# The first seven steps of a table of complex powers taken from angles and magnitudes, and one doubling step in place

## The chip, the core and the metric

The program runs on one core of one Trainium2 chip. The metric is device time in microseconds (us). Its engines are named as in the profile: PE (TensorE matmul), PEld (TensorE weight load), DVE (VectorE), ACT (ScalarE), POOL (GpSimd) and SP (SyncE, which here issues nearly all DMAs). One kernel computes two independent halves of a result and shares every engine between them.

## The reference

Half A is a Fourier mixing layer on x [2048, 512], with matrices given as inputs. Half B is a long convolution of u [2048, 512] whose taps come from 128 decaying oscillations for each of 512 channels.

```python
a = x @ dft_hid_re.T ; b = x @ dft_hid_im.T
ya = dft_seq_re @ a - dft_seq_im @ b

dt = exp(log_dt)
A = -exp(log_A_real) + 1j * A_imag            # [512, 128]
C = (C_real + 1j * C_imag) * dt[:, None]
P = exp((A * dt[:, None])[:, :, None] * arange(2048))
K = 2.0 * einsum("dn,dnl->dl", C, P).real     # taps, [512, 2048]
yb = causal convolution of u with K along the sequence (by FFTs of length 4096) + u * D_skip
out = concatenate([ya, yb], axis=-1)
```

All of it is float32. The expensive part of B besides the FFTs is P: powers 0 to 2047 of 512 x 128 complex numbers.

## The kernel before

**Order.** A small planner in the kernel file (`Plan`) records the instructions. Each piece of work is a generator that names an engine and an assumed duration before it issues an instruction, and waits for events and counted resources (`Sem`). The planner takes the piece that can start first, then the one of lower "urgency". Its result is one fixed order for each engine; the hardware then only waits on semaphores. A change of assumed durations, urgencies or resources therefore moves instructions on all engines.

**Half A** (`Fnet`) uses the symmetry of the DFT matrices. Four groups t = 0 to 3 of 512 output rows, two parts c each, four tiles k each make 32 loads of 1 MB ("quads", `load_quad`); DVE folds each into `rest` (lines 444 and 449), ACT squares it for a numerical guard (line 473), PE multiplies (`sums`, lines 556 and 559), ACT keeps the sums, and PE makes the second product (`outputs`, lines 655 and 656: four column blocks e of each group, for each of them four k, one f32 and one bf16 matmul of 512 columns, called a pair below). `FNET` holds the urgencies of the four groups; `GROUP_US`, `QUAD_US` and `AHEAD_US` say how early in the plan the loads may begin.

**Half B** (`Ssm`) works in 16 chunks of 32 channels; the 128 partitions are the 128 oscillations. For each chunk two tables are built. The first (`tables1`, tile `t1t`) holds C·A^(64m) for m = 0 to 31. The second (`tables2`, tile `t2`) holds A^l for l = 0 to 31, and `top` holds what stands for l = 32 to 63. PE multiplies both (`taps`, line 1219) into the 2048 taps of each channel. Two chunks make a 64-channel stage of the first FFT step (`stage1_k`). Then, for units of 128, 128, 128, 64 and 64 channels, follow products with the spectrum of u (`product`: line 1461, ACT copies, DVE lines 1491 and 1493, and the matmuls of line 1507) and inverses (`inverse`, line 1578). Intermediate arrays go through DRAM. The last chunk and the last unit have paths of their own (`last_stage1_k`, `last_unit`, lines 1267, 1273, 1476, 1479).

**Seeds.** `seed_args` makes, for one or two chunks at a time (`PAIRS`), the arguments A^(2^j), j = 0 to 10, as magnitudes and angles in the tile `seed` [3, 11, channels]: five copies with a scale on ACT (lines 1046 and 1048), the reduction of the angles on DVE (lines 1050 and 1052), then Abs, Exp and three Sin on ACT with two loads of function tables (lines 1054 to 1062). `seeds` multiplies magnitude with cosine and sine (DVE, line 1072, 704 elements a partition) into `cs`, and ACT adds a copy with signs (line 1078). One `seed` tile exists (`res`, a resource of 1); it is given back when the last chunk's `seeds` has read it.

**Tables.** A table is doubled step by step: `mul` multiplies the rows that are there by a seed (line 997, both real products at once, into a scratch tile `prod` or `prod2`), `add` combines them into new rows (line 1006). In the second table rows 1, 2 and 4 are first copied from `cs` by ACT (lines 1146 and 1149), row 3 comes from row 1 and rows 5 to 7 from rows 1 to 3 (two `mul`, two `add`); even rows from 8 on come from squares (lines 1013, 1026, 1032), odd ones from `mul` and `add`, and `top` from lines 1020, 1167 and 1171. In the first table the last doubling (rows 0 to 15 into 16 to 31) is done by `halves`: `mul` and `add` on the first 16 channels and then on the other 16, because `prod` holds 1024 elements.

## Time and profile before

| | |
|---|---|
| median of 3 runs | 479.33 us (477.11 to 482.01) |
| the profiled execution | 480.8 us, span 479.0 us, mean granted TensorE clock 0.953 |
| PE busy | 398.7 us (83%) |
| DVE busy | 424.7 us (89%) |
| ACT busy | 320.1 us (67%) |
| POOL busy | 1.4 us |
| DMA | 112.52 MB, mean 235 GB/s |

The span is the time from the first to the last instruction of the profiled execution; its own time is 1.8 us more. Rows of a group give a line, an engine, an operation, out<-in with the program's tile names and shapes, the count, then busy us and mean ns of one, then idle time of that engine just ahead of it and what ended it. Rows of the timeline give start, duration, engine, line, operation, tiles, shape and count; where a row stands for several instructions the duration runs from the first start to the last end.

### The profile page before, as it was taken

The page shows a single profiled execution, that of the slowest core. Times are in us where ns is not written, and L with a number is a line of the kernel's source. Part 1 is how long each engine was busy: PE and PEld are TensorE (multiplying, and loading weights), DVE is VectorE, ACT ScalarE, POOL GpSimd, SP SyncE. Part 2 cuts the span into 40 slices and gives each one's busy share as a digit, 9 for nine tenths or more (in the row PEclk, how much of TensorE's full clock was granted, in tenths as well). Part 3 has the DMA queues.
Part 4 walks back from the last instruction along what each step waited for, and adds up shares of the span by engine and source line. Part 5 has one row for each costly group of instructions (what it writes and reads, how often), then busy time and mean ns, then how long its engine had stood idle before and what let it go on. Part 6 is the DMA issues. An engine that isn't in the chain of part 4 may idle for free. (4 is left out here: it accounts for less than half of the span.)

```text
span 479.0 us, 13676 instructions
## 1 busy us (share of the span) xinstructions
PE 398.7 (83%) x5739; PEld 210.9 (44%) x5778; DVE 424.7 (89%) x718; ACT 320.1 (67%) x603; POOL 1.4 (0%) x15
## 2 busy tenths in 40 slices
PE   3669869999987989699898698987988789778593
PEld 3123213435422535264353563544447346456283
DVE  2999998899999998998999999999999999991433
ACT  1537889997796557966798587589748847253231
POOL 0000000000000000000000000000000000000000
PEclk8979879999997999999999999999998999999689
DMA  8995759967888789998867799439462966959575
GB/s 309 387 370 190 249 213 316 322 221 264 229 289 276 273 238 313 296 297 269 252 200 232 246 278 260 110 88 273 133 220 57 272 140 199 242 118 254 187 200 114
DMA packets 128002, 112.52 MB, mean 235 GB/s; under 512 B 53568, under 2 KB 97984, under 8 KB 127424
## 3 DMA queue, kind: packets, MB, share of 16 engines
q1 hardware_dynamic: 119968, 108.58, 74.2%
q10 hardware_dynamic: 7968, 3.02, 2.6%
q8 instruction: 47, 0.77, 0.7%
q14 instruction: 19, 0.16, 0.1%
HBM read 78.09 MB, written 33.49 MB: 233 GB/s over the span
## 5 line engine op out<-in xcount | busy, mean ns | idle before, releaser
L997 DVE TENSOR_TENSOR prod<-tables,cs 128x1024 f32<-128x1024 f32 (+4 forms) x160 | 123.5, 797 | 3.3 <-ACT tables L1146 3.0
L655 PE MATMUL f<-p,w 128*128 128x512 f32 x128 | 68.1, 614 | 6.4 <-ACT y L681 5.2
L1006 DVE TENSOR_TENSOR tables<-prod 128x512 f32<-128x512 f32 (+4 forms) x160 | 72.1, 475 | 0.1
L473 ACT ACTIVATE slots<-rest 128x1536 f32<-128x1536 bf16 x28 | 41.5, 1483 | 17.0 <-DVE rest L444 9.3
L1219 PE MATMUL f<-tables 128*32 128x96 f32 x2048 | 46.3, 247 | 5.1 <-DVE tables L1273 1.4
L444 DVE TENSOR_TENSOR rest<-slots,base 128x512 bf16<-128x512 f32 (+2 forms) x44 | 46.1, 1049 | 3.7 <-DMA slots<-in_sT 2.8
L556 PE MATMUL f<-base,es 128*128 128x512 f32 x64 | 37.1, 664 | 13.9 <-ACT es L357 7.1
L1219 PEld LDWEIGHTS f<-tables 128*32 128x32 f32 x2048 | 42.3, 110 | 12.7 <-issue 6.3
L1171 DVE TENSOR_TENSOR tables<-tables,cs 128x1024 f32<-128x1024 f32 x32 | 38.1, 1219 | 0.0
L655 PEld LDWEIGHTS f<-p,w 128*128 128x128 f32 x128 | 22.6, 191 | 32.1 <-issue 20.9
L556 PE MATMUL f<-base,ec 128*128 128x512 f32 x64 | 35.4, 635 | 0.1
L854 ACT ACTIVATE big<-f 128x512 f32<-128x512 f32 x36 | 20.2, 597 | 15.7 <-PE f L1295 7.9
L1486 ACT ACTIVATE big<-f 128x1024 f32<-128x1024 f32 x24 | 23.6, 1017 | 10.0 <-PE f L1461 9.1
L1461 PE MATMUL f<-big,w 64*32 64x256 f32 (+1 forms) x832 | 24.3, 363 | 7.1 <-DMA big<-xk 5.1
L559 PE MATMUL f<-rest,xi 128*128 128x512 bf16 x86 | 26.6, 402 | 3.8 <-DVE rest L444 2.3
L559 PE MATMUL f<-rest,xr 128*128 128x512 bf16 x87 | 25.7, 390 | 4.2 <-DVE rest L444 2.0
L854 ACT ACTIVATE mid<-f 128x512 f32<-128x512 f32 x24 | 13.0, 591 | 16.2 <-PE f L1507 16.2
L1243 ACT ACTIVATE ks<-f 128x256 f32<-128x256 f32 (+3 forms) x26 | 13.8, 557 | 14.6 <-PE f L1219 14.5
L556 PEld LDWEIGHTS f<-base,es 128*128 128x128 f32 x64 | 11.8, 205 | 26.0 <-ACT es L357 8.1
L1295 PE MATMUL f<-ks,f1k 32*128 32x512 f32 (+1 forms) x224 | 22.5, 527 | 0.1
L1507 PE MATMUL f<-big,ia 32*64 32x256 f32 x384 | 17.5, 409 | 6.1 <-DVE big L1493 3.2
L1461 PEld LDWEIGHTS f<-big,w 64*32 64x32 f32 x832 | 14.9, 106 | 16.6 <-issue 11.0
(191 smaller groups left out, 702.6 us busy)
## 6 DMA issues: line engine op xcount, KB each, us to landing
slots<-in_sT SPq DMA_DIRECT2D x28, 768.0 KB, 7.1
xu<-big SPq DMA_DIRECT2D x16, 512.0 KB, 5.5
base<-in_sT SPq DMA_DIRECT2D x31, 256.0 KB, 6.2
xk<-big SPq DMA_DIRECT2D x6, 1024.0 KB, 7.0
big<-xu SPq DMA_DIRECT2D x12, 512.0 KB, 7.2
big<-xk SPq DMA_DIRECT2D x12, 512.0 KB, 7.6
zs<-mid SPq DMA_DIRECT2D x10, 512.0 KB, 5.4
big<-zs SPq DMA_DIRECT2D x10, 512.0 KB, 5.7
```

Source lines behind the costliest of these rows:

```text
L444: return v.tensor_tensor(rest[:, lo:hi:step], raw[:, lo:hi:step], base[:, None, :].to_broadcast([128, n, DM]), op=op)
L473: nc.scalar.activation(raw, rest, AF.Square, accum_out=self.stat[:, n:n + 1])
L556: nc.tensor.matmul(out, x[:, cols], base, start=k == 0, stop=False)
L559: nc.tensor.matmul(out, still[:, cols], rest[:, h], start=False, stop=k == 3 and h == 2)
L655: nc.tensor.matmul(ps, self.w[k][:, cols], self.p[t, c][:, d], start=k == 0, stop=False)
L854: self.nc.scalar.activation(to, src, AF.Copy)
L997: self.nc.vector.tensor_tensor(p.rearrange("p k d c m -> p k (d c) m"), src.rearrange("p d c l -> p (d c) l")[:, None, :, rows].to_broadca ...
L1006: self.nc.vector.tensor_tensor(dst[:, :, :, rows], p[:, 0], p[:, 1, :, ::-1], op=OP.add)
L1171: self.nc.vector.tensor_tensor(self.top[:, :, k, ::1 - 2 * k, 16:32], t[:, :, :, 1:32:2], cs[:, k, 5, :, :, None].to_broadcast([128, CHUNK ...
L1219: nc.tensor.matmul(ps[32 * j:32 * j + 32, i], t1[:, d, c], t2[:, :, d, c], start=c == 0, stop=c == 1, tile_position=(0, 32 * j))
L1461: nc.tensor.matmul(both[:, :, c], self.w2[rows, R * q + r, xx, 32 * c:32 * c + 32], xs[rows, r, xx], start=True, stop=True, tile_position= ...
L1486: a.activation(flat[:, 1024 * m:1024 * m + 1024], p.rearrange("p b d -> p (b d)"), AF.Copy)
```

## The change

The angles and magnitudes are made for fifteen powers instead of eleven: 1 to 7 and then 8, 16, ... 1024, and the tile `seed` is turned round to [3, channels, 15], so that the fifteen values of one channel lie side by side. A new process `direct` multiplies magnitude by cosine and sine for the powers 1 to 7 straight into rows 1 to 7 of the second table (one DVE instruction of 448 elements). The ACT copies into rows 1, 2 and 4 and the two `mul` and two `add` that made rows 3 and 5 to 7 are gone. `seeds` now makes the eight powers from 8 on (512 elements instead of 704), and reads them across the channels, 15 elements apart. `seed_args` issues nine scaled copies on ACT instead of five (`POWERS`), and its other instructions cover 15 values a channel instead of 11.

The resource `res` becomes two halves of the tile; it is given back when both the `seeds` and the `direct` of all its chunks have read it (`took_seeds`). The groups are now chunk 0, chunk 1, and then seven pairs, instead of chunk 0, seven pairs, and chunk 15.

The last doubling of the first table is done by `in_place` for all chunks but the last: one product into `prod` (1024 elements), one product straight into the new rows (1024), one addition in place (1024), instead of two products of 1024 and two additions of 512.

Three planner constants differ: `FNET` 2.0 becomes 1.5 for all groups, `GROUP_US` 29 becomes 37, `AHEAD_US` 35 becomes 15.

```diff
-        self.kss, self.res = Sem(1), Sem(1)
+        self.kss, self.res = Sem(1), Sem(2)
...
+    def in_place(self, name, t, rows, seed, to, between=()):
+        d, m = t.shape[1], len(range(64)[rows])
+        n = 2 * d * m
+        p = self.tab.tile([128, 1024], F32, name=name)[:, :n].rearrange("p (d c m) -> p d c m", d=d, c=2)
+        for k, out in ((1, p), (0, t[:, :, :, to])):
+            yield "dve", dve(n), *APART[:2 * bool(between or not k)]
+            self.nc.vector.tensor_tensor(out, t[:, :, :, rows], seed[:, k, :, :, None].to_broadcast([128, d, 2, m]),
+                                         op=OP.mult)
+        yield from between
+        yield "dve", dve(n), *APART[:2 * bool(between)]
+        self.nc.vector.tensor_tensor(t[:, :, :, to], t[:, :, :, to], p[:, :, ::-1], op=OP.add)
...
-        yield self.res
-        s = self.tab.tile([128, 3, 11, 2 * CHUNK], F32, name="seed")[:, :, :, :w]
+        for _ in range(PAIRS[g][1]):
+            yield self.res
+        o = CHUNK if g == 1 else 0
+        s = self.tab.tile([128, 3, 2 * CHUNK, 15], F32, name="seed")[:, :, o:o + w]
...
-        a.activation(args[:, :, 0], par[:, 0:2], AF.Copy)
-        for j in (1, 2, 4, 8):
-            a.activation(args[:, :, j:min(2 * j, 11)], args[:, :, 0:min(j, 11 - j)], AF.Copy, scale=2.0 ** j)
-        yield "dve", dve(n, 2)
+        for steps in POWERS:
+            yield "act", sum(0.1 + 2 * w * len(range(15)[to]) * 0.00083 for to, _, _ in steps) + 0.09
+            for to, of, scale in steps:
+                a.activation(args[:, :, :, to], par[:, 0:2, :, None] if of is None else args[:, :, :, of], AF.Copy,
+                             scale=scale)
+        n = 15 * w
...
+    def took_seeds(self, g):
+        self.seeds_left[g] -= 1
+        if not self.seeds_left[g]:
+            for _ in range(PAIRS[g][1]):
+                self.plan.put(self.res)
+
     def seeds(self, g, j, s):
         yield self.css
-        s = s[:, :, :, CHUNK * j:CHUNK * j + CHUNK]
-        cs = self.tab.tile([128, 2, 11, CHUNK, 2], F32, name="cs", bufs=2)
-        yield "dve", dve(22 * CHUNK)
-        self.nc.vector.tensor_tensor(cs[:, :, :, :, 0], s[:, 1:3], s[:, 0:1].to_broadcast([128, 2, 11, CHUNK]),
+        s = s[:, :, CHUNK * j:CHUNK * j + CHUNK, 7:].rearrange("p n d l -> p n l d")
+        cs = self.tab.tile([128, 2, 8, CHUNK, 2], F32, name="cs", bufs=2)
+        yield "dve", dve(16 * CHUNK)
+        self.nc.vector.tensor_tensor(cs[:, :, :, :, 0], s[:, 1:3], s[:, 0:1].to_broadcast([128, 2, 8, CHUNK]),
...
-            yield from self.halves("prod", t, slice(0, 16), cs[:, :, 10], slice(16, 32), n == 15 and self.t1_half)
+            if n == 15:
+                yield from self.halves("prod", t, slice(0, 16), cs[:, :, 7], slice(16, 32), self.t1_half)
+            else:
+                yield from self.in_place("prod", t, slice(0, 16), cs[:, :, 7], slice(16, 32))
...
+    def direct(self):
+        for n in range(16):
+            yield "urgency", 2 + FIRST_TABLE * n + DIRECT
+            yield self.box_ev[n]
+            yield self.lent_ev
+            yield self.t2s
+            if n == 15:
+                self.plan.spawn(self.last_unit(), 1)
+            g, j, seeds = self.box.pop(n)
+            seeds = seeds[:, :, CHUNK * j:CHUNK * j + CHUNK, :7]
+            yield "dve", dve(14 * CHUNK)
+            self.nc.vector.tensor_tensor(self.t2[n % 2][:, :, :, 1:8].rearrange("p d c l -> p c d l"), seeds[:, 1:3],
+                                         seeds[:, 0:1].to_broadcast([128, 2, CHUNK, 7]), op=OP.mult)
+            self.took_seeds(g)
+            self.plan.set(self.low_steps[n])
...
             yield self.cs_ev[n]
-            yield self.lent_ev
-            yield self.t2s
+            yield self.low_steps[n]
...
-            yield "act", act(2 * CHUNK), ahead
-            a.activation(t[:, :, :, 1].rearrange("p d c -> p c d"), cs[:, :, 0, :, 0], AF.Copy)
-            for c in range(2):
-                yield "act", act(2 * CHUNK), ahead
-                a.activation(t[:, :, c, 2:6:2].rearrange("p d j -> p j d"), cs[:, c, 1:3, :, 0], AF.Copy)
-            p = yield from self.mul("prod2", t, slice(1, 2), cs[:, :, 1])
-            yield from self.add(p, t, slice(3, 4))
-            p = yield from self.mul("prod2", t, slice(1, 4), cs[:, :, 2])
-            yield from self.add(p, t, slice(5, 8))
...
-PAIRS = ((0, 1), *((n, 2) for n in range(1, 15, 2)), (15, 1))
+PAIRS = ((0, 1), (1, 1), *((n, 2) for n in range(2, 16, 2)))
-FNET, GUARD, XTS = (2.0, 2.0, 2.0, 2.0), 2, 2
+FNET, GUARD, XTS = (1.5, 1.5, 1.5, 1.5), 2, 2
-GROUP_US, QUAD_US, AHEAD_US = 29, 7.0, 35
+GROUP_US, QUAD_US, AHEAD_US = 37, 7.0, 15
```

What this does to the order is shown at three places. In the rows below, a name such as prod_2833 is the scratch tile of the second table, prod without a number that of the first; the line numbers of the changed program are 13 to 41 higher from `in_place` on (L1006 became L1019, L1072 L1095, L1171 L1207, L1461 L1497, L1491 L1527, L1578 L1614).

DVE before, in the middle of the program: the end of the tenth chunk's second table (L1167, L1171) and the first seeds that are read from a newly filled `seed` tile (L1072, for the twelfth chunk). The reduction of the angles of that group's tile (L1052) stands eight rows ahead of the first row shown.

```order
L1032 TENSOR_TENSOR tables<-square 128x32x4
L1006 TENSOR_TENSOR tables<-prod_2833 128x64x4
L997 TENSOR_TENSOR prod_2852<-tables,cs 128x1024
L1026 SCALAR_TENSOR_TENSOR tables<-tables 128x32x8
L1032 TENSOR_TENSOR tables<-square 128x32x8
L1006 TENSOR_TENSOR tables<-prod_2852 128x64x8
L1167 SCALAR_TENSOR_TENSOR tables<-tables 128x32x16
L1171 TENSOR_TENSOR tables<-tables,cs 128x64x16
L1171 TENSOR_TENSOR tables<-tables,cs 128x32x2x16
L997 TENSOR_TENSOR prod<-tables,cs 128x128
L1072 TENSOR_TENSOR cs<-seed 128x704
```

DVE now, also at the end of the tenth chunk's tables, which is the turn to a new pair: the reduction of the new pair's angles (L1068), the last rows of the tenth chunk, and the first instruction that reads the new seeds, the direct product of the eleventh chunk (L1178).

```order
L1068 TENSOR_TENSOR seed<-seed 128x960
L1019 TENSOR_TENSOR tables<-prod 128x64x8
L1039 SCALAR_TENSOR_TENSOR tables<-tables 128x32x8
L1010 TENSOR_TENSOR prod<-tables,cs 128x1024
L1010 TENSOR_TENSOR tables<-tables,cs 128x64x16
L1045 TENSOR_TENSOR tables<-square 128x32x8
L1014 TENSOR_TENSOR tables<-tables,prod 128x64x16
L1019 TENSOR_TENSOR tables<-prod_2594 128x64x8
L1203 SCALAR_TENSOR_TENSOR tables<-tables 128x32x16
L1207 TENSOR_TENSOR tables<-tables,cs 128x64x16
L1207 TENSOR_TENSOR tables<-tables,cs 128x32x2x16
L1178 TENSOR_TENSOR tables<-seed 128x2x32x7
```

Between the reduced angles and the first instruction that reads the finished tile there were seventeen rows, and there are ten now; the tile's next filling begins only after the last L1178 of its chunks.

DVE before, behind the last table row of the last chunk (the second L1171): products of the third and fourth unit (L1491, L1493), and the transposes (L1273) that empty the PSUM banks of the last chunks' first FFT step.

```order
L1171 TENSOR_TENSOR tables<-tables,cs 128x32x2x16
L1491 TENSOR_TENSOR slots<-big_105 128x512
L1493 TENSOR_TENSOR big_105<-big_105 128x2x256
L1491 TENSOR_TENSOR mid_108<-slots 128x512
L1273 STREAM_TRANSPOSE tables<-f_4518 128x2x8x32
```

DVE now, at the same place.

```order
L1207 TENSOR_TENSOR tables<-tables,cs 128x32x2x16
L1527 TENSOR_TENSOR mid_108<-big_107 128x512
L1309 STREAM_TRANSPOSE tables<-f_4280 128x2x8x32
L1529 TENSOR_TENSOR big_107<-big_107 128x2x256
L1309 STREAM_TRANSPOSE tables<-f_4284 128x2x8x32
```

One product row stands ahead of the first transpose instead of three.

PE before, directly ahead of the last chunk's taps: a product of the third unit (L1461, 2x128), the last pair of half A's output (L655, L656) and the first product of the fourth unit (2x64); behind the taps PE has no more work of half A.

```order
L1461 MATMUL f_4455<-big_105,w_98 32x2x128 x16
L1461 MATMUL f_4456<-big_105,w_98 32x2x128 x16
L655 MATMUL f_4253<-p_3169,w_518 128x512
L656 LDWEIGHTS v_551
L656 MATMUL f_4253<-low_3360,v_551 128x512
L1461 MATMUL f_4498<-slots,w_98 32x2x64 x32
```

PE now, behind the last chunk's taps: inverse pieces of the second unit (L1614), both products of the fourth unit (L1497, two rows each), and the first of eight pairs of half A's last two output blocks.

```order
L1614 MATMUL f_4468<-big_105,ib 64x128 x8
L1497 MATMUL f_4470<-big_106,w_98 32x2x64 x32
L1497 MATMUL f_4505<-big_106,w_98 32x2x64 x32
L1614 MATMUL f_4468<-big_105,ib 64x128 x8
L655 MATMUL f_4508<-p_3643,w_245 128x512
L656 LDWEIGHTS v_387
L656 MATMUL f_4508<-low_3722,v_387 128x512
L1497 MATMUL f_4586<-tables,w_98 32x2x64 x32
L1497 MATMUL f_4597<-tables,w_98 32x2x64 x32
L655 MATMUL f_4508<-p_3643,w_410 128x512
```

Behind the last taps there stood three 64-channel products (L1461), five double groups of L1507 and eight groups of L1578; now there are four, five and twelve, and the eight pairs of half A, spread between the products and groups of the last two units.

39 lines of the change are left out of this document (23 added, 16 removed).

## Prediction

> **What bounds the kernel now.** I read the page's busy times first, then the busy time by stage, then who waited for whom on DVE. The chain of waits is of no use here: it ends after one instruction of 0.1%.
>
> ```profile
> PE 398.7 (83%) x5739; PEld 210.9 (44%) x5778; DVE 424.7 (89%) x718; ACT 320.1 (67%) x603; POOL 1.4 (0%) x15
> DVE  2999998899999998998999999999999999991433
> ```
>
> The digits show DVE near full from the second to the 36th of 40 slices and mostly idle in the last four. So the kernel has two parts, and the stages are cut at the end of the last table row on DVE, the end of the last taps on PE, and the last matmul:
>
> ```profile
> core 0: us, PE busy (x) PEld busy (x) DVE busy (x) ACT busy (x) POOL busy (x), PEclk, DMA share, GB/s
> 12.00:425.68 413.68, 358.21 (x4623) 178.96 (x4664) 399.43 (x684) 302.58 (x573) 0.53 (x1) 0.96 0.78 239
> 432.33:474.17 41.84, 31.64 (x936) 24.07 (x936) 15.47 (x20) 13.51 (x23) 0.00 (x0) 0.88 0.72 196
> ```
>
> Up to 425.68 us DVE works 399.43 of 413.68 us: what it saves there comes off, as long as nothing makes it wait. From 432.33 to 474.17 it works 15.47 of 41.84 us; there PE is the busiest, with 31.64 us and 10.2 us idle. DVE's waits in the first part are few:
>
> ```profile
> DVE prod L997 <- ACT tables L1146: 3.0, 3, 1.7
> DVE rest L444 <- DMA slots<-in_sT: 2.8, 4, 1.3
> ```
>
> **What an instruction costs DVE.** The groups by shape give durations, the timeline gives starts:
>
> ```profile
> L997 DVE TENSOR_TENSOR prod<-tables,cs 128x1024 f32<-128x1024 f32 x64 | 77.5, 1217 | 0.1
> L1006 DVE TENSOR_TENSOR tables<-prod 128x512 f32<-128x512 f32 x64 | 43.7, 683 | 0.0
> L997 DVE TENSOR_TENSOR prod<-tables,cs 128x128 f32<-128x128 f32 x32 | 11.9, 379 | 3.0 <-ACT tables L1146 3.0
> L1006 DVE TENSOR_TENSOR tables<-prod 128x128 f32<-128x128 f32 x16 | 4.6, 288 | 0.1
> L997 DVE TENSOR_TENSOR prod<-tables,cs 128x384 f32<-128x384 f32 x16 | 8.9, 554 | 0.0
> L1006 DVE TENSOR_TENSOR tables<-prod 128x192 f32<-128x192 f32 x16 | 5.6, 352 | 0.0
> L1052 DVE TENSOR_TENSOR seed<-seed 128x704 f32<-128x704 f32 x7 | 6.2, 883 | 0.0
> L1050 DVE TENSOR_SCALAR seed<-seed 128x704 f32<-128x704 f32 x7 | 3.7, 522 | 0.0
> ...
> 299.26 0.89 DVE L1072 TENSOR_TENSOR cs<-seed 128x704 f32<-128x704 f32 x1
> 300.06 0.28 DVE L1006 TENSOR_TENSOR tables<-prod 128x64 f32<-128x64 f32 x1
> 300.19 0.72 DVE L997 TENSOR_TENSOR prod<-tables,cs 128x128 f32<-128x128 f32 x2
> 300.83 0.42 DVE L1006 TENSOR_TENSOR tables<-prod 128x64 f32<-128x64 f32 x2
> ...
> 321.26 2.35 DVE L1171 TENSOR_TENSOR tables<-tables,cs 128x1024 f32<-128x1024 f32 x2
> 323.53 0.37 DVE L997 TENSOR_TENSOR prod<-tables,cs 128x128 f32<-128x128 f32 x1
> ```
>
> Between 1024 and 512 elements the duration falls by 534 ns: 1.04 ns an element. Two of 1024 start 1.135 us apart (323.53 less 321.26, halved), 0.08 us less than one lasts, so an instruction takes its elements' time and 0.07 us. By that the 512 take 0.60 us, the 704 0.80 (300.06 less 299.26), the 384 0.47, the 192 0.27, the 64 0.13, and a 128 of line 997 0.32 (0.64 for two).
>
> **The change on DVE, part by part.** For each chunk the two products and two additions of rows 3 and 5 to 7 go: 0.32 + 0.13 + 0.47 + 0.27 = 1.19 us, 19.0 us for 16 chunks. The seeds fall from 704 to 512 elements: 0.20 us, 3.2 us in all. The direct product of 448 elements costs 0.07 + 0.47 = 0.54 us, 8.6 us in all. The angle reduction grows from 704 to 960 elements for a pair: 0.27 us for the subtraction, and 0.13 us for the rounding, which runs at two elements in that time (522 ns for 704); 0.40 us for seven pairs and half of it for two single chunks are 3.2 us. The last doubling takes three instructions of 1.135 instead of two of 1.135 and two of 0.60: 0.06 us less, 15 times, 0.9 us. Together 11.3 us less.
>
> The trace does not show the new reading of the seeds: both operands step 15 elements (60 bytes) from one to the next. One end is no excess: line 1072 now writes 8 bytes apart and its 0.80 us is 704 elements at the usual rate. The nearest row in kind is the 128-element product of line 997, which reads one element of each 32-element table row, 128 bytes apart: 379 ns against 288 for an addition of 128, 0.71 ns an element more. For 512 elements that is 0.36 us, 5.8 us in all; 11.7 us if both operands pay one after the other; 0 if that row pays for its inner length of one, not for the distance. I take half of 5.8, 2.9 us, because the row allows either reading, and keep 0 and 11.7 for the range.
>
> [...]
>
> **Waits.** The three ACT copies into the table go, and with them 3.0 us of DVE waiting. What can take their place is the seed chain:
>
> ```profile
> 330.26 0.89 DVE L1052 TENSOR_TENSOR seed<-seed 128x704 f32<-128x704 f32 x1
> 331.24 0.79 ACT L1054 ACTIVATE seed<-seed 128x704 f32<-128x704 f32 x1 [0.70 <-DVE seed L1052]
> 336.54 0.87 ACT L1062 ACTIVATE seed<-seed,halfpi 128x704 f32<-128x704 f32 x1
> ```
>
> From 331.24 to 337.41 ACT needs 6.2 us; 256 more elements in each of four steps add about 0.9 us, as 704 take 0.8. The tile is now held until the direct product of the pair's second chunk, so the next filling starts later: ten DVE rows stand behind the reduction in the place shown, some 8 us by the prices above, where seventeen stood. 7.1 us and ACT's other work in between leave next to nothing. I take 0.4 us of waiting for each of seven pairs, 3 us, between 0 and 8. It cancels the 3.0.
>
> DVE therefore ends its tables 11.3 - 2.9 = 8.4 us earlier. The taps behind them follow 1.2 us closer: they waited for a transpose ahead of which three 512-element products stood, and now one, 0.60 us each. Their end moves from 432.3 to 422.7 us.
>
> **The end of the program.** The order now puts behind the last taps what PE had done before them:
>
> ```profile
> 417.71 0.38 PE L656 MATMUL f<-low,v 128*128 128x512 bf16 x1
> 418.79 0.38 PE L656 MATMUL f<-low,v 128*128 128x512 bf16 x1
> 446.59 1.90 PE L1461 MATMUL f<-tables,w 64*32 64x128 f32 x94 [3.42 <-issue]
> 456.83 2.55 PE L1461 MATMUL f<-tables,w 64*32 64x128 f32 x128
> 459.32 1.09 PE L1578 MATMUL f<-tables,ib 128*64 128x128 f32 x16
> 471.18 1.15 PE L1578 MATMUL f<-tables 128*64 128x64 f32 x32 [1.69 <-issue]
> 473.02 1.15 PE L1578 MATMUL f<-tables 128*64 128x64 f32 x32 [0.69 <-ACT tables L854]
> ```
>
> Eight pairs of half A at 1.08 us (418.79 less 417.71) are 8.6 us, one more 64-channel product 2.5, four more inverse groups at 1.09 are 4.4: 15.5 us more PE work, added to 31.64. Against that stand PE's 10.2 us idle, of which 3.4 are the one gap ahead of 446.59. The pairs lie just there, between products, and are long matmuls; the idle time near the end (1.69 us before 471.18, 0.69 before 473.02) has nothing to fill it. I take 7.1 of the 10.2 us as filled: this part grows by 8.4 us, between 5.3 (all filled) and 15.5 (none).
>
> **Sum.** -8.4 (DVE) - 1.2 (taps) + 8.4 (end) = -1.2 us. In the second table an addition and the product behind it more seldom stand next to each other now that four short dependent steps are gone; I count 0 for it, up to 2 us less. The profiled execution's 480.8 us become 479.6; it lies 1.5 us above the median of the runs, so 478.1 us. With the up to 2 us at half, 477 us.
>
> **Rivals.** Results within about 1% (474.5 to 484.1 us) cannot be told from no change here.
>
> *Forecast*, the end gives back most of what DVE saves: 477, own range 472 to 481. For it speaks the order at the end, against it that PE's pairs may fill more. Chance 0.43.
>
> *The saving stays.* Strided reading costs nothing, the seed chain keeps clear and all of PE's idle time is filled: 479.3 - 11.3 - 3.0 - 1.2 - 2 + 5.3 = 467 us. For it speaks that all removed instructions lie where DVE is full; with one of the three missing it is 470 to 473. Chance 0.31.
>
> *The end grows by its full work.* PE's idle time is "issue", not lack of work; if each short product brings its own gap as before 446.59, the end grows 15.5 us: 477 + 7.1 = 484 us. It ends slower than before as soon as that stretch grows by more than 10.7 us. Chance 0.16.
>
> [...] Chance 0.10. [...]
>
> **Range and chances.** Faster by over 1%: 0.28 of the second case and 0.11 of the first, 0.39. Slower by over 1%: 0.08 of the third, 0.07 of the fourth, 0.15, and 0.02 of the first. Within 1%: 0.44. From 467 to 485 us about 2 in 10 are left out.
>
> **What would show it.** Line 1095's 512 elements at 684 ns: free; near 1.05 us: one operand pays; 1.4: both. Idle time ahead of lines 1066, 1095 and 1178 is the seed chain. The last row of line 1207 should start near 416 us, and the last taps end near 423. PE from there to its last matmul should take 50 us with 47 busy. If that stretch stays near 42 us, or the last table row comes after 422 us, the prediction is wrong in that step.

## The result, and the profile after

The changed kernel takes 484.82 us (median of 12 runs, 480.20 to 489.57), the kernel before, run beside it, 479.00 (12 runs, 477.11 to 483.08). The ratio is 1.0119, with a 95% interval of 1.0083 to 1.0154: slower by 1.2%, some 5.7 us. The forecast was 477.0, no change or a little faster; the time lies at the upper end of its range of 467 to 485. The profiled execution took 486.56 us, with a span of 484.8. In the experiments E5, E9 and E11 the profiled execution was one of that kernel's longer ones, so the lengths of its stages are not used.

First the busy times and the DVE digits of the page after, which answer to those of before (DVE 424.7 us in 718 instructions):

```profile
span 484.8 us, 13631 instructions
PE 405.9 (84%) x5778; PEld 212.0 (44%) x5778; DVE 417.0 (86%) x655; ACT 330.7 (68%) x591; POOL 1.4 (0%) x15
DVE  3999998899999998999899999999999997934260
```

DVE has 7.7 us less to do, PE 7.2 us more busy time, and the span is 5.8 us longer. The busy time by stage of the changed kernel, cut at the end of the last table row on DVE, the end of the last taps and the last matmul as before:

```profile
core 0: us, PE busy (x) PEld busy (x) DVE busy (x) ACT busy (x) POOL busy (x), PEclk, DMA share, GB/s
12.00:420.86 408.86, 350.25 (x4446) 171.36 (x4448) 390.25 (x617) 308.43 (x554) 0.53 (x1) 0.94 0.74 232
427.38:479.47 52.09, 46.22 (x1152) 32.45 (x1152) 18.62 (x26) 18.28 (x30) 0.00 (x0) 0.93 0.86 231
```

The first stage ends 4.8 us earlier than before (420.86 for 425.68), the last taps 4.95 us earlier (427.38 for 432.33). The stretch behind them takes 52.09 us instead of 41.84: PE works 14.6 us more there and is idle 5.9 us instead of 10.2. So in this pair of executions the first stage gains 4.8 us, and the end takes twice as much back.

The instructions of the change, by shape:

```profile
L1095 DVE TENSOR_TENSOR cs<-seed 128x512 f32<-128x512 f32 x16 | 16.9, 1056 | 0.2 <-ACT seed L1078 0.2
L1178 DVE TENSOR_TENSOR tables<-seed 128x448 f32<-128x448 f32 x16 | 9.9, 617 | 1.9 <-ACT seed L1078 1.9
L1068 DVE TENSOR_TENSOR seed<-seed 128x960 f32<-128x960 f32 x7 | 8.1, 1151 | 0.0
L1066 DVE TENSOR_SCALAR seed<-seed 128x960 f32<-128x960 f32 x7 | 4.6, 657 | 3.1 <-ACT seed L1062 3.1
```

The direct product and the angle reduction cost what was worked out. The seeds of line 1095 take 1056 ns where 512 neighbouring elements take 684: 0.37 us more each, 6.0 us in all.

The longest waits that are new or grown (engine and line, for whom; us in total, times, longest), of DVE and of PE:

```profile
DVE tables L1045 <- ACT square L1026: 5.2, 4, 2.4
DVE seed L1066 <- ACT seed L1062: 3.6, 6, 1.0
...
PE f L1255 <- DVE tables L1207: 9.5, 1, 9.5
```

DVE's waits for ACT up to the last table row add up to 12.6 us where they were 6.0. PE stands 9.5 us ahead of the taps of the sixth chunk, which the new order puts in its queue before their table is done.

Last, the rows on PE in the last stretch that the experiments turn on, and its busy time in two slices of 4 us there:

```profile
436.53 1.09 PE L1614 MATMUL f<-big,ib 128*64 128x128 f32 x14
439.71 0.38 PE L1614 MATMUL f<-big,ib 128*64 128x128 f32 x2 [2.09 <-issue]
440.02 1.58 PE L655 MATMUL f<-p,w 128*128 128x512 f32 x2
441.96 3.37 PE L1497 MATMUL f<-tables,w 64*32 64x128 f32 x128
...
445.25 1.12 PE L655 MATMUL f<-p,w 128*128 128x512 f32 x2
450.78 2.03 PE L1497 MATMUL f<-tables,w 64*32 64x128 f32 x128
```

```profile
436.00:440.00 4.00, 1.91 (x59) 1.31 (x45) 2.68 (x4) 1.72 (x2) 0.00 (x0) 1.00 0.94 209
440.00:444.00 4.00, 4.00 (x84) 2.48 (x90) 0.00 (x0) 0.60 (x1) 0.00 (x0) 0.57 1.12 265
```

In the middle of a group of 16 like matmuls PE stops for 2.09 us and waits for nothing that the profile shows. In the 4 us after that the granted clock is 0.57, and the next product takes 3.37 us where the same product later takes 2.03.

### The profile page after: what moved, and what is told of

Same layout as the page of the kernel before. It is cut to its first block, busy times and chain, and to the rows that moved or that the text cites. A ratio compares the mean times of both kernels' runs of the same rounds, so it can differ in the third digit from the quotient of the medians.

```text
span 484.8 us, 13631 instructions
## 1 busy us (share of the span) xinstructions
PE 405.9 (84%) x5778; PEld 212.0 (44%) x5778; DVE 417.0 (86%) x655; ACT 330.7 (68%) x591; POOL 1.4 (0%) x15
## 5 line engine op out<-in xcount | busy, mean ns | idle before, releaser
L655 PE MATMUL f<-p,w 128*128 128x512 f32 x128 | 70.1, 630 | 6.8 <-ACT y L681 6.8
L997 DVE TENSOR_TENSOR prod<-tables,cs 128x1024 f32<-128x1024 f32 (+3 forms) x98 | 74.3, 774 | 1.7 <-ACT cs L1100 1.2
L1255 PE MATMUL f<-tables 128*32 128x96 f32 x2048 | 49.4, 255 | 13.8 <-DVE tables L1207 9.5
L1255 PEld LDWEIGHTS f<-tables 128*32 128x32 f32 x2048 | 45.3, 114 | 23.1 <-issue 11.8
L1019 DVE TENSOR_TENSOR tables<-prod 128x256 f32<-128x256 f32 (+3 forms) x98 | 44.0, 463 | 0.0
L1207 DVE TENSOR_TENSOR tables<-tables,cs 128x1024 f32<-128x1024 f32 x32 | 38.3, 1218 | 0.0
L655 PEld LDWEIGHTS f<-p,w 128*128 128x128 f32 x128 | 22.3, 193 | 32.3 <-issue 19.1
L559 PE MATMUL f<-rest,xi 128*128 128x512 bf16 x96 | 28.7, 407 | 1.8 <-DVE xi L273 1.0
L1062 ACT ACTIVATE seed<-seed 128x128 f32<-128x128 f32 (+2 forms) x72 | 28.0, 456 | 0.9
L1497 PE MATMUL f<-big,w 64*32 64x256 f32 (+1 forms) x832 | 25.1, 369 | 3.4 <-DMA big<-xk 1.4
L1026 ACT ACTIVATE square<-tables 128x256 f32<-128x256 f32 (+1 forms) x32 | 16.5, 517 | 14.8 <-DVE tables L1178 11.4
L656 PE MATMUL f<-low,v 128*128 128x512 bf16 x64 | 24.8, 387 | 0.0
L593 PE MATMUL f<-base,bec 128*128 128x512 bf16 x32 | 13.7, 504 | 12.5 <-ACT p L619 11.5
L559 PEld LDWEIGHTS <-xi 128*128 128x128 bf16 x96 | 9.7, 102 | 28.1 <-issue 23.3
```

The lines of the kernel that those rows point to most:

```text
L559: nc.tensor.matmul(out, still[:, cols], rest[:, h], start=False, stop=k == 3 and h == 2)
L655: nc.tensor.matmul(ps, self.w[k][:, cols], self.p[t, c][:, d], start=k == 0, stop=False)
L997: self.nc.vector.tensor_tensor(p.rearrange("p k d c m -> p k (d c) m"), src.rearrange("p d c l -> p (d c) l")[:, None, :, rows].to_broadca ...
L1019: self.nc.vector.tensor_tensor(dst[:, :, :, rows], p[:, 0], p[:, 1, :, ::-1], op=OP.add)
L1062: a.activation(args[:, :, :, to], par[:, 0:2, :, None] if of is None else args[:, :, :, of], AF.Copy, scale=scale)
L1207: self.nc.vector.tensor_tensor(self.top[:, :, k, ::1 - 2 * k, 16:32], t[:, :, :, 1:32:2], cs[:, k, 2, :, :, None].to_broadcast([128, CHUNK ...
```

## The experiments

Ratios are against the kernel before, run beside each, with 95% intervals; 1% is 4.8 us. The stage rows below are cut at the start of the last table row, at the end of the last taps and at the end of the last matmul.

### E1: the old planning numbers

```diff
-FNET, GUARD, XTS = (1.5, 1.5, 1.5, 1.5), 2, 2
+FNET, GUARD, XTS = (2.0, 2.0, 2.0, 2.0), 2, 2
-GROUP_US, QUAD_US, AHEAD_US = 37, 7.0, 15
+GROUP_US, QUAD_US, AHEAD_US = 29, 7.0, 35
```

> The changed kernel with the three planning numbers of before (2.0, 29 and 35 in place of 1.5, 37 and 15); all work is done. Theory A (the loss lies in what stands behind the last taps, and it is the shorter DVE work, not these numbers, that moves work there): the order still puts eight pairs of half A and 288 product matmuls behind the last taps, so the last table row starts near 420 us, the stretch from the last taps to the last matmul stays between 50 and 54 us, and the time between 481 and 488 us. Rival B (the new planning numbers are at fault): the stretch falls back towards 42 us and the time to 474 to 478 us.

Measured: 492.09 us, ratio 1.0238 (1.0154 to 1.0322). The last table row starts at 417.62 us, the last stretch takes 56.72. Rival B falls: with the old numbers the changed kernel is slower still. The stretch and the time are longer even than Theory A had them (50 to 54 us, 481 to 488).

### E2: the higher seeds side by side by channel

```diff
+        low = args[:, :, :7 * w].rearrange("p n (d l) -> p n l d", l=7)
+        high = args[:, :, 7 * w:].rearrange("p n (l d) -> p n l d", d=w)
...
-        s = s[:, :, CHUNK * j:CHUNK * j + CHUNK, 7:].rearrange("p n d l -> p n l d")
+        s = s[:, :, 7 * w:].rearrange("p n (l d) -> p n l d", d=w)[:, :, :, CHUNK * j:CHUNK * j + CHUNK]
```

> The changed kernel, its order on DVE and PE unchanged row for row, with the eight higher powers of a seed tile stored power by power, so that line 1095's product reads neighbouring elements; the seven low powers stay side by side for each channel; all work is done. Theory A (strided reading costs 0.37 us a seed product, and DVE's end sets the start of the last stretch): the seed product falls from 1056 ns to about 684, the 16 of them by 6.0 us, the last table row starts near 414 us instead of 419.65, the last stretch stays near 52 us, and the time falls by 5 to 6 us to about 479. Rival C (PE, behind with its own work, sets the end whatever DVE does): the last table row starts earlier but the stretch behind grows by the same, and the time falls by less than 2 us. Rival D (the seed's ACT work comes late now): idle time ahead of the seed products takes up half of it or more, and the time is 481 to 483.

Measured: 481.79 us, ratio 1.0082 (1.0028 to 1.0136). The seed product's group, DVE's longest wait, and the first and last stage of this kernel:

```profile
L1100 DVE TENSOR_TENSOR cs<-seed 128x512 f32<-128x512 f32 x16 | 11.1, 691 | 0.0
...
DVE seed L1070 <- ACT seed L1067: 6.1, 7, 1.4
```

```profile
12.00:417.49 405.49, 343.79 (x4363) 173.18 (x4409) 383.53 (x617) 308.74 (x552) 0.52 (x1) 0.94 0.74 233
425.66:477.80 52.14, 44.59 (x1147) 31.53 (x1152) 18.67 (x26) 18.27 (x30) 0.00 (x0) 0.93 0.87 229
```

The stride is the whole price: 691 ns instead of 1056, 5.8 us off DVE. But the ratio falls only from 1.0119 to 1.0082, 1.8 us (3.0 by the medians), and the two intervals overlap. Something else moved too: ACT's copies into the new layout became dearer (23 of them take 572 ns instead of 496), and DVE's wait for them ahead of the rounding (line 1070, 1066 in the changed kernel) grew from 3.6 to 6.1 us. In the first stage DVE is busy for 5.5 us less and idle for 3.4 us more. That is Rival D in part, one step earlier than it said: nothing waits ahead of the seed products themselves. The stretch behind the last taps stays where it was, 52.14 us, so Rival C's mechanism is not seen, although the fall of the ratio is of its size.

### E3: the late pairs left out

```diff
                 cols = slice(128 * e, 128 * e + 128)
+                if t == 3 and e > 1:
+                    if k == 0:
+                        nc.tensor.matmul(ps, self.w[k][:, cols], self.p[t, c][:, d], start=True, stop=True)
+                    continue
```

> The changed kernel without 15 of the 16 matmuls of the eight pairs of half A that stand behind the last taps (of the last 512 rows, the output's last two blocks of 128 columns: their first matmul stays); nothing else moves. Theory A (that stretch is bound by PE, and the pairs lie on its path): 15 matmuls at about 0.57 us are 8.5 us of PE work; the stretch falls from 52.1 to 44 to 47 us and the time to 477 to 479 us. Rival E (the pairs fill time in which PE would wait anyway, and the stretch is long for another reason): PE's busy time there falls by 8.5 us but its idle time grows by 6 or more, and the time stays between 482 and 485 us.

Measured: 483.12 us, ratio 1.0043 (1.0005 to 1.0080). The last stretch, and three of the rows on PE in it:

```profile
423.28:474.05 50.77, 38.91 (x1133) 28.00 (x1132) 18.73 (x26) 18.05 (x30) 0.00 (x0) 0.97 0.89 236
```

```profile
437.14 0.38 PE L1618 MATMUL f<-big,ib 128*64 128x128 f32 x2 [2.92 <-issue]
442.06 0.41 PE L1501 MATMUL f<-tables,w 64*32 64x128 f32 x4 [1.56 <-issue]
447.92 1.29 PE L1501 MATMUL f<-tables,w 64*32 64x128 f32 x69 [2.50 <-issue]
```

The edit leaves one matmul of each of the two blocks, so 14 of the 16 are gone. PE's busy time in the stretch falls by 7.3 us, the stretch by 1.3; PE's unexplained stops grow instead, inside groups of like matmuls. Over all runs the kernel is 1.7 us (medians) to 3.6 us (ratios, whose intervals just part) shorter than the changed one. So Rival E is right in the main: the pairs cost the end a half of their length at most. (Up to the last taps this kernel issues the same instructions as the changed one, yet its last table row started at 415.65 us instead of 419.65: single executions differ by that much, which is why stages are compared here only where the difference is larger or is repeated.)

### E4: the order of a slower DVE

```diff
-            yield "dve", dve(14 * CHUNK)
+            yield "dve", dve(14 * CHUNK) + 1.0
```

> The changed kernel, with the planner told that the direct product of each chunk takes 1.0 us longer than it does (16 us in all, about what the change takes off DVE); every instruction is the same, only the order differs: behind the last taps stand one pair instead of eight, 128 product matmuls instead of 256 and 96 inverse matmuls instead of 128. Theory A (the saving is real and is given back by the order at the end): the last table row starts near 420 us as in the changed kernel, the stretch behind the last taps takes 38 to 43 us with some 30 busy, and the time is 471 to 476 us, under the kernel before. Rival C (PE has no room before the last taps, so that pulling its work ahead of them makes the taps late by the same): the last taps end near 432 us or later and the time stays at 480 to 485 us.

Measured: 489.95 us, ratio 1.0177 (1.0112 to 1.0241). Its three stages:

```profile
12.00:433.51 421.51, 359.94 (x4660) 179.24 (x4699) 394.84 (x624) 314.24 (x562) 0.53 (x1) 0.94 0.77 237
433.51:448.05 14.54, 13.62 (x314) 8.73 (x315) 5.84 (x8) 3.09 (x5) 0.00 (x0) 1.00 0.73 201
448.05:486.24 38.19, 27.14 (x746) 21.67 (x747) 13.11 (x17) 10.88 (x20) 0.00 (x0) 0.88 0.59 153
```

The end is as short as ordered, 38.19 us. But the work that was pulled ahead of the taps makes them 20 us later: the last table row starts at 433.51, with DVE idle for 26.7 of 421.5 us, and PE is busy for nearly all of the 14.5 us behind it. Theory A in its first form falls with this run: in this order, at least, moving PE's work forward does not bring the saving. It is Rival C's mechanism, at a time beyond its range; the 3 us by which the ratio exceeds that of the changed kernel are within the intervals.

### E5, E9, E10, E14, E15: one engine after the other relieved, in the order of before

E5 leaves out the two products and two additions whose removal is the heart of the change, and moves nothing else. E9 leaves out PE work, E10 both, E15 adds ACT to E5, E14 relieves all three.

```diff
(DVE)
-            p = yield from self.mul("prod2", t, slice(1, 2), cs[:, :, 1])
-            yield from self.add(p, t, slice(3, 4))
-            p = yield from self.mul("prod2", t, slice(1, 4), cs[:, :, 2])
-            yield from self.add(p, t, slice(5, 8))
+            for n4 in (128, 64, 384, 192):
+                yield "dve", dve(n4)
(PE)
+                if t < 3 and e < 3 and k in (1, 2):
+                    continue
(ACT)
-        nc.scalar.activation(raw, rest, AF.Square, accum_out=self.stat[:, n:n + 1])
+        nc.scalar.activation(raw[:, 0, :128], rest[:, 0, :128], AF.Square, accum_out=self.stat[:, n:n + 1])
```

> The kernel before, its order unchanged row for row, without the two products and two additions that make rows 3 and 5 to 7 of each chunk's second table (those rows hold zeros, set once by GpSimd); the ACT copies into the table stay. That takes 1.19 us a chunk, 19.0 us in all, off DVE and moves nothing on PE. Theory A (DVE sets the table stage, and only the changed order loses the gain): the last table row starts near 407 us instead of 424, the last stretch stays near 42 us, and the time falls to 460 to 465 us. Rival C (PE has hardly any room before the last taps, so that DVE is not alone in setting the stage): DVE's new idle time is spent waiting for PE, for buffers that PE frees or for half A's steps, the last table row comes at 416 us or later, and the time is 471 to 477 us.

> The kernel before, order unchanged, without 18 of half A's output pairs (of the first three groups of 512 rows, the first three blocks of 128 columns: the two middle ones of four pairs each); all of them stand in the table stage, and 18 at 1.08 us are 19.4 us off PE; DVE keeps all its work. Theory C (PE and DVE bind the table stage together, each waiting now and then for the other): the last table row comes 2 to 6 us earlier and the time is 473 to 477 us. Rival A (DVE alone binds it): within 2 us of the kernel before.

> Both reliefs at once in the order of the kernel before: 19.0 us off DVE (rows 3 and 5 to 7 of the second tables left at zero) and 19.4 us off PE (the same 18 pairs left out). Theory C: what the one engine alone could not turn into time now comes through; the time falls by 13 to 19 us, more than the two reliefs alone together, to 461 to 468 us. Rival I (a third thing holds the stage, the transfers or the in-order queues themselves): no more than the sum of the two alone, 470 us or more.

> The kernel before, order unchanged, with 19.0 us off DVE (rows 3 and 5 to 7 of the second tables at zero), 19.4 us off PE (18 output pairs of half A left out) and now some 34 us off ACT (the guard's sums over 128 columns). Theory K: with the third engine relieved the 19 us come through, and the time falls to 458 to 466 us. Rival L: no more than 3 us below the 473 us of the two reliefs.

> The kernel before, order unchanged, with 19.0 us off DVE and some 34 us off ACT, PE untouched. Theory K with PE as the next bound: between the 475 us of DVE's relief alone and 466 us. Rival L: 473 to 477 us, as with DVE's relief alone.

| run | taken off, as priced | ratio | interval |
|---|---|---|---|
| E5 | DVE 19.0 us | 0.9854 | 0.9769 to 0.9939 |
| E9 | PE 19.4 | 0.9938 | 0.9897 to 0.9978 |
| E10 | DVE 19.0, PE 19.4 | 0.9845 | 0.9777 to 0.9914 |
| E15 | DVE 19.0, ACT 34 | 0.9879 | 0.9822 to 0.9935 |
| E14 | all three | 0.9888 | 0.9832 to 0.9943 |

With DVE relieved the kernel gains 1.1 to 1.6%, some 5 to 7.5 us, whatever else is relieved. E5's Theory A (460 to 465 us) falls; its 475.24 us are Rival C's. E9, PE relieved alone, gains 0.6%, some 3 us, a little more than its Rival A allowed. The stage up to the last table row, in E10, E14 and E15 in this order (before: 412.45 us long, PE busy 358.03 at clock 0.96, DVE 398.20):

```profile
12.00:421.11 409.11, 351.76 (x4604) 177.60 (x4602) 384.55 (x618) 300.65 (x571) 1.41 (x3) 0.92 0.77 241
```

```profile
12.00:420.58 408.58, 349.19 (x4567) 177.65 (x4602) 384.59 (x619) 265.20 (x571) 1.41 (x3) 0.92 0.78 241
```

```profile
12.00:419.44 407.44, 357.76 (x4619) 178.05 (x4656) 385.19 (x618) 265.25 (x571) 1.41 (x3) 0.95 0.78 242
```

Three things can be read. Of the 19.0 us priced, 13 to 13.7 arrive as less DVE busy time. The traces show why: most DVE instructions start 0.08 us before the one ahead has ended, but in the kernel before 54 of the stage's 682 start right behind its end, and in E10, E14 and E15 108 to 110 do. The new ones are nearly all an addition behind its own product, or a product behind the addition whose rows it reads: the instructions left out had stood between them. Some 55 times 0.08 us are 4.4 of the missing 5.3 to 6 us. Second, only 3.3 to 5 us of those 13 shorten the stage; DVE's idle time grows from 14.2 to between 22 and 25 us. (The rest of E10's gain lies in its last stretch, 36.90 us, whose instructions are those of before: the stages of single executions differ by several us, the ratios of whole runs are the firmer figure.) Third, PE's relief was given back through the granted clock. E14 and E15 differ by PE's relief alone: 19.4 us less work take 8.6 us off PE's busy time (357.76 to 349.19), and 357.76 less 19.4 is 338.4 us at 0.95, which at 0.92 is 349. What lowers the clock the runs do not show; in the last stretch of the changed kernel a stop of 2.09 us stood ahead of the 4 us at 0.57.

Theory C of E10 and Theory K fall: beside DVE's relief, 19.4 us off PE and 34 us off ACT change nothing that can be measured. Rival I stands: DVE's relief brings what it brings alone, and neither PE nor ACT is what holds the rest back.

### E7 and E8: the new numbers alone, the doubling alone

```diff
(E7, kernel before)
-FNET, GUARD, XTS = (2.0, 2.0, 2.0, 2.0), 2, 2
+FNET, GUARD, XTS = (1.5, 1.5, 1.5, 1.5), 2, 2
-GROUP_US, QUAD_US, AHEAD_US = 29, 7.0, 35
+GROUP_US, QUAD_US, AHEAD_US = 37, 7.0, 15
(E8, kernel before)
-            yield from self.halves("prod", t, slice(0, 16), cs[:, :, 10], slice(16, 32), n == 15 and self.t1_half)
+            if n == 15:
+                yield from self.halves("prod", t, slice(0, 16), cs[:, :, 10], slice(16, 32), self.t1_half)
+            else:
+                yield from self.in_place("prod", t, slice(0, 16), cs[:, :, 10], slice(16, 32))
```

> The kernel before with the three planning numbers of the changed one (1.5, 37 and 15); all work is done. The order behind the last taps keeps its counts (no pair of half A, 192 product and 96 inverse matmuls). Theory A and rival C alike (the numbers are not what loses): within 4 us of the kernel before. Rival B (the numbers are at fault): 483 us or more.

> The kernel before with one part of the change alone: the last doubling of the first table in place (three instructions of 1024 elements instead of two of 1024 and two of 512, 15 times); all work is done. On DVE that is 0.9 us less. Because the planner works out the order anew, behind the last taps now stand 256 product and 128 matmuls of the next step instead of 192 and 160. Theory A: 477 to 480 us. Rival H (any renewed order moves the time by several us, whatever the edit saves): more than 3 us away from the kernel before, in either direction.

Measured: E7 481.96 us, ratio 1.0024 (0.9975 to 1.0073); E8 493.82 us, ratio 1.0235 (1.0143 to 1.0326). In the kernel before the three numbers change no instruction and no place in any queue, so E7 only shows how well two runs of one program agree; its last table row starts at 427.22 us, 2.8 us later than in the profiled execution of before. E8 is the sharpest result of all: an edit that takes 0.9 us off DVE costs 11 us, and what else differs is the order that the planner writes. Its stages up to the last two table rows (the last one starts at 431.95) and behind the last taps:

```profile
12.00:430.81 418.81, 368.73 (x4590) 181.69 (x4592) 396.96 (x668) 299.95 (x570) 0.53 (x1) 0.95 0.76 235
439.08:489.10 50.02, 35.72 (x1000) 27.92 (x1000) 18.42 (x24) 14.58 (x23) 0.00 (x0) 0.81 0.58 158
```

Rival H is right in this run: DVE's busy time on the page is 0.6 us down (424.1 for 424.7), and both stages are longer, the last one with a granted clock of 0.81. The new doubling does not wait on itself: up to the last table rows DVE's longest waits are for PE (5.0 us ahead of line 444) and for ACT (4.0 us ahead of line 997), those for DVE's own rows 0.5 us.

### E6: half the product instructions at the end

```diff
+                        if w == 64:
+                            if r % 2:
+                                continue
...
+                            nc.tensor.matmul(both[:, :, :, c], self.w2[rows, R * q + r, xx, 32 * c:32 * c + 32],
+                                             xs[rows, r:r + 2, xx], start=True, stop=True, tile_position=(64 * g, 32 * xx))
```

> The changed kernel, order unchanged, where each two matmuls of the 64-channel products of 128 columns are one of 256 columns (with the weights of the first of the two, so that half of these products is computed with other weights). PE streams the same columns, with 128 matmul and 128 weight-load records less of the 2304 behind the last taps. Theory F (PE is paced there by the arrival of its instructions: the third run of the first set took 7.3 us of PE's busy time away in 30 instructions and the stretch fell by 1.3 us, while 10 or 11 instruction transfers of 16 KB are counted in the last 55 us): one transfer of some 256 instructions less, the stretch falls by 3.5 to 5 us, to 47 to 48.5, and the time by as much. Rival G (the stretch is set by the chain of products, evacuations, stores and loads): it stays within 1.5 us of 52.1, the time within 2 us of the changed kernel's.

Measured: 480.79 us, ratio 1.0019 (0.9978 to 1.0060), 4.8 us less than the changed kernel, and the intervals do not touch. The last stretch and the product in which PE had stopped:

```profile
425.66:473.84 48.18, 42.61 (x897) 27.39 (x896) 18.64 (x26) 18.02 (x30) 0.00 (x0) 1.00 0.92 247
```

```profile
433.49 1.70 PE L1500 MATMUL f<-big,w 64*32 64x256 f32 x49 [0.40 <-issue]
435.11 1.09 PE L1623 MATMUL f<-big,ib 128*64 128x128 f32 x16
```

The group of 16 that had stopped for 2.09 us now runs through. The trace counts 255 matmul records fewer (and 256 weight loads), twice what was expected, since each of these matmuls leaves two (the two order rows of x32 of such a product are 128 records on PE in the timeline). Executions of the same stretch without this edit took 52.14 us (E2), 52.36 (E13) and 50.56 (E16). PE's unexplained stops in the stretch fall from 3.7 us (0.19, 2.09, 0.37 and 1.08) to 1.7, the granted clock rises from 0.93 to 1.00, and PE's busy time falls by 3.6 us with nearly the same columns to stream. Theory F gave the time, by more than its own mechanism: of the 3.9 us, 2.0 are stops that went, 3.6 are busy time, most of it the clock, and 1.6 came back as a new wait for ACT.

That the stops are late instructions is inferred from the traces, which hold every 16 KB instruction transfer with its start and length:

| run | PE goes on at | after a stop of | an instruction transfer had ended at |
|---|---|---|---|
| changed | 439.71 | 2.09 | 438.01 |
| E2 | 439.36 | 2.91 | 437.89 |
| E13 | 437.19 | 2.91 | 435.76 |
| E3 | 437.14 | 2.92 | 435.79 |
| E3 | 442.06 | 1.56 | 440.48 |
| E3 | 447.92 | 2.50 | 446.63 |
| before | 441.10 | 1.50 | 439.49 |
| before | 446.59 | 3.42 | 445.08 |

The first four are one place in the program, the middle of the same group of 16. In the last stretches of before, the changed kernel, E2, E3, E6, E13 and E16, all nineteen unexplained stops of 0.4 us or more ahead of the last 100 weight loads end 1.2 to 1.7 us behind the end of such a transfer, while the transfers come several us apart (in the changed kernel their ends lie 3.4 to 6.3 us apart). And the stops lie 127 or 128 weight loads apart, or a multiple of that; with their matmuls these are some 256 records. E6 has 511 records fewer, and 7 transfers in the stretch instead of 9.

### E11, E13, E16, E17: relief in the changed kernel, and fewer bytes

```diff
(E11: the product and the addition of the step m = 8)
+                if m == 8:
+                    yield "dve", dve(16 * CHUNK)
(E13: ACT's sums over 128 columns, as above; E16, E17: also)
-                queue.dma_start(raw, self.sT[t, c, k, 1:].rearrange("h p t -> p h t"))
+                few = 1 if place >= 8 else 3
+                queue.dma_start(raw[:, :few], self.sT[t, c, k, 1:1 + few].rearrange("h p t -> p h t"))
```

> The changed kernel, order unchanged, without the product and the addition that make rows 9, 11, 13 and 15 of each second table (zeros, set once by GpSimd): 0.60 and 0.33 us a chunk, 14.9 us off DVE. Theory C: DVE's relief is worth about a third here too; the last table row starts 3 to 6 us earlier than 419.65, the stretch behind the last taps stays at 52 us, and the time is 478 to 482 us. Rival A: the last table row starts near 405 and the time is 468 to 472 us.

> The changed kernel, order unchanged, where ACT's sum of squares over each quarter of half A's matrix (a guard's figure, not part of the result) takes 128 columns instead of 1536: 32 times 1.48 us become about 0.41, some 34 us off ACT, and the raw tiles come free for the next loads that much earlier. Theory K (ACT's queue, which evacuates PE's results and makes the squares and seeds that DVE waits for, is the third engine that holds the table stage): DVE's and PE's waits for ACT in the table stage (12.6 and 41.5 us in the changed kernel) fall by a third or more, the last table row starts at 413 us or earlier, and the time falls by 5 us or more, to 479 or less. Rival L (the waits for ACT are waits for work that ACT itself waits for, PE's or DVE's, passed on): the time stays within 2 us of the changed kernel.

> The thirteenth run's kernel (the changed one, order unchanged, with ACT's guard sums over 128 columns), where 24 of the 28 later loads of half A's matrix bring a third of their 768 KB; the other two thirds keep what the buffer held, so that half A multiplies by stale numbers. That is 12.6 of 112.6 MB less. Theory M (the transfers, 74 to 78% busy through the table stage and in order on one queue, are the thing that holds it): the time falls by 6 us or more below the thirteenth run's, to 478 or less, and the last table row starts at 411 us or earlier. Rival N (no further single thing holds it; each of DVE's waits is a short one for another neighbour in the fixed order): within 3 us of the thirteenth run's.

> The fifteenth run's kernel (the one before, order unchanged, with 19.0 us off DVE and some 34 us off ACT) with the same 12.6 MB less to load. Theory M: DVE's relief comes through, 464 to 469 us. Rival N: within 3 us of the fifteenth run's 475, in either direction.

Measured: E11 480.66 us, ratio 0.9996 (0.9955 to 1.0038), 5.9 us less than the changed kernel for 14.9 us off DVE. E13 483.72 us, 1.0056 (1.0006 to 1.0106); E16 481.22 us, 1.0095 (1.0054 to 1.0136); E17 473.21 us, 0.9903 (0.9853 to 0.9953), where E15 had 0.9879. So DVE's relief is worth about 0.4 here too. 34 us less of ACT work is worth 1 us by the medians and 3 by the ratios (the interval overlaps that of the changed kernel), 12.6 MB fewer to load nothing that can be measured. Theories K and M fall; Rivals L and N are not contradicted.

### E12: another order, with the seeds of E2

```diff
-ARGS = 0.3
+ARGS = 1.0
-FIRST_TABLE, T1, SEEDS = 0.01, -0.005, 1.5
+FIRST_TABLE, T1, SEEDS = 0.01, 0.005, 1.5
-GROUP_US, QUAD_US, AHEAD_US = 37, 7.0, 15
+GROUP_US, QUAD_US, AHEAD_US = 31, 7.0, 25
```

> The changed kernel with the higher seeds stored power by power, as in the second run of the first set, in another order: planning numbers 31 and 25 in place of 37 and 15, the first table's step of a chunk ranked just behind the second's instead of just ahead (0.005 for -0.005), and the seed chains ranked later (1.0 for 0.3); all work is done. Behind the last taps stand seven pairs of half A and 192, 128 and 96 small matmuls, where the kernel before has 192, 160 and 96 and the changed one 256, 160 and 128. Theory J (a microsecond off DVE is worth 0.3 to 0.4, so the 11 us that this version takes off are worth some 4; the rest of the difference is what the order puts behind the last taps): the last stretch takes 42 to 46 us and the time is 474 to 480 us, at or under the kernel before. Rival H (any renewed order costs several us somewhere): the stretch is short, but the last table row comes after 425 us, and the time is 484 us or more.

Measured: 483.36 us, ratio 1.0080 (1.0040 to 1.0119). Its three stages, the first cut at the start of the last two table rows (the last one starts at 420.91):

```profile
12.00:419.77 407.77, 351.98 (x4333) 172.95 (x4376) 381.00 (x608) 307.96 (x552) 0.53 (x1) 0.93 0.77 237
419.77:439.70 19.93, 16.60 (x491) 11.49 (x492) 15.33 (x20) 8.54 (x13) 0.00 (x0) 0.91 0.99 222
439.70:477.68 37.98, 33.18 (x889) 23.25 (x893) 15.84 (x21) 13.41 (x23) 0.00 (x0) 1.00 0.67 198
```

The last stretch is short, 37.98 us with seven pairs in it, and the tables are done early; but now PE's work stands between them, and the last taps end 18.79 us behind the start of the last table row instead of 7.73. Neither theory held as put: the end is shorter than Theory J had it and the time above its range, and the last table row comes earlier than Rival H said. No version tried here that does all the work beats the kernel before.

## Why the prediction was wrong

**The sum, term by term.** The forecast had -9.4 us in the first stage (-8.4 on DVE and 1 for its neighbours), -1.2 for the taps and +8.4 at the end, -2.2 in all. The two profiled executions have -4.8, -0.15 and +10.25, and 0.5 behind the last matmul: +5.8. So 4.6 of the 8.0 us lie in the first stage, 1.05 in the taps and 1.85 in the end. In the first stage the forecast of DVE's work came out, by luck in part (see below): it is busy for 389.0 us up to the start of the last table row instead of 398.2. What failed there is the term that was put at nothing, the waits: DVE's idle time grew from 14.25 to 18.6 us. This split rests on one pair of executions. E7, the program of before, starts its last table row at 427.22 us, and E3 and E6, with the changed kernel's instructions up to there, at 415.65 and 417.72, so the first stage gained between 4.8 and 11.6 us. The end is longer in every execution: 50.6 to 52.4 us (the changed kernel, E2, E13, E16) against 36.9 to 41.8 (before, E7, E10, E14, E15).

**Where the time goes.** From the start of the last table row to the last matmul the kernel before needs 49.7 us, the changed one 59.8, E2 60.3, E1 66.4, E12 56.8, E8 57.2, E4 52.7; the row itself starts at 424.5, 419.7, 417.5, 417.6, 420.9, 432.0 and 433.5. The orders that get the tables done earlier have more of PE's work left behind them, the one whose end is nearly as short as before (E4) has the latest tables, and E8 has both late tables and a long end. None of the orders tried has both an early last row and a short end.

**"What it saves there comes off, as long as nothing makes it wait."** This first step failed. In an unchanged order 13 us less of DVE busy time shorten the kernel by 5 to 7.5 us (E5, E10, E14, E15), 14.9 priced us by 5.9 (E11), 5.8 us by 1.8 (E2, where ACT's copies became dearer): a third to somewhat over a half. So the 7.7 us by which DVE's busy time fell are worth some 2.5 to 4, before any order is counted. What takes the rest is not one engine. Beside DVE's relief, relieving PE and ACT and cutting the bytes added nothing that can be told from none, and DVE's idle time grew instead in waits of under 10 us each for PE, ACT and the transfers in turn. That the fixed order itself, with each queue standing in line, is what holds the stage is argued from this, not shown.

**Seeds.** I took half of the row's price, 2.9 us; the row was right, 6.0 us. Both operands together pay what one strided operand of the row paid: 0.73 ns an element here, 0.71 there. E2 shows it is the stride: 691 ns with the elements side by side, 1056 with 60 bytes from one to the next.

**Waits.** The forecast was 3.0 us gone and 3 us of seed chain come. The seed chain cost 5.5 us (3.6 ahead of line 1066, 1.9 ahead of line 1178). The term that was missing is the square that ACT makes for line 1045: 5.2 us where 2.1 stood before. The longest, 2.4 us, is seen in ACT's rows of the changed kernel's timeline:

```profile
407.88 0.60 ACT L854 ACTIVATE big<-f 128x512 f32<-128x512 f32 x1 [6.22 <-PE f L1331]
408.38 0.41 ACT L1026 ACTIVATE square<-tables 128x256 f32<-128x256 f32 x1
```

ACT's order is fixed, and an evacuation that waited 6.22 us for PE stood ahead of the square. All DVE's waits for ACT in the stage grew by 6.6 us in this pair, from 6.0 to 12.6, not by nothing; in other executions of the same instructions they are 8.1 (before, in E7) and 9.6 and 11.6 (changed, in E3 and E6).

**The sum on DVE.** Forecast -8.4 us, measured -7.7 on the whole page. This is luck in part: with the seeds at 6.0 the terms give -5.3. The "up to 2 us" for neighbours, of which the sum took half, is seen: 30 of the stage's DVE instructions start right behind the end of the one ahead where 54 did, and 24 times 0.08 are some 2 us. The last table row was forecast near 416 us; in three executions of these instructions it started at 419.65, 415.65 (E3) and 417.72 (E6).

**Taps "1.2 us closer".** From the start of the last table row to the last taps' end it is 7.73 us instead of 7.88: a gain of 0.15.

**The end.** Forecast +8.4 us, measured +10.25 (52.09; 52.14 in E2). The work was sized well (15.5 us forecast, 14.6 measured); of 7.1 us of idle time only 4.3 were filled. But the reason was only half right. The pairs, about half of that work, are nearly free in the profiled execution (E3: 1.3 of 7.3 us; over all runs 1.7 to 3.6), and the other 7 us of small matmuls bring most of the growth. The small matmuls there had a price beside their columns: stops that end 1.2 to 1.7 us behind an instruction transfer (E6), and behind the stop of 2.09 us 4 us at a granted clock of 0.57 (behind one of 2.92 us in E3 it stayed at 1.00). The gap of 3.42 us ahead of 446.59, which the forecast took for room to fill, is such a stop: an instruction transfer had ended at 445.08. The pairs did shorten such stops: without them they come to 8.9 us in E3, where the changed kernel has 2.7. The 16 KB instruction transfers in the stretch number 8 before, 9 after and 7 in E6, and 9 in E3, whose stretch is hardly shorter.

**Rivals.** The time, 484.8, is that of "the end grows by its full work" (484). Its own condition, over 10.7 us of growth, was just missed, and its mechanism is right only in that the idle time was "issue": the stops come with every 127 or 128 weight loads at most, not with each product. That its time came out is luck in part. That the seeds pay on both operands, one after the other, the fourth case with a chance of 0.10, no run shows: 11.7 us stood for it, and 6.0 were measured (1056 ns an instruction, not 1.4 us). "The saving stays" is excluded as well. No case of mine had the one that mattered most: that a microsecond off the busiest engine is worth a third to somewhat over a half of one, and that a new order can cost more than the edit saves. E1 moved by 6 us from the changed kernel and E8 by 11 from the one before, through order; E4's 3 us are within the intervals.

## What to carry to other kernels

An engine busy for 97% of a stage need not be what sets it, as DVE here (398.2 of 412.45 us): before counting a saving at full price, leave the same work out in the unchanged order and see what comes through. Where a planner writes the order, price the order as a change of its own, since even an edit of under a microsecond can make it another one; look at what now stands behind the last step of the long stage, and count there instructions as well as columns. Two operands that step 60 bytes from one element to the next cost half as much again here (1056 ns, for 691 in E2), and if the layout suits one of two readers, store each part as its own reader wants it (E2: 5.8 us of DVE time for a change of view).
